# Two spectral-and-MLP layers on one core: rest transposes moved to other banks, stores moved to another queue, and four small changes of order

## The chip, the cores and the metric

The kernel runs on one core of a Trainium2 chip. The core has five engines that run beside one another, each in its own program order: TensorE (PE in the profile, its weight loads PEld), VectorE (DVE), ScalarE (ACT), GpSimd (POOL) and SyncE (SP). They meet at semaphores. TensorE writes its sums into PSUM, which has eight banks here; an engine that wants to write into a bank waits for the readers of what was there. Transfers between the chip's memory and the core's on-chip memory are issued by an engine's queue: almost all here by SP's, a few by ACT's. A queue takes its transfers in order, and one that waits for its data holds back those behind it.

The metric is the device time of one execution in microseconds (us), lower is better. A difference of 0.2%, which is 5.4 us here, is about what a measurement of this kernel can tell from no change.

## The reference, cut to what matters

```python
# S = 2048 tokens, D = 576, F = 4608, float32, one batch
def A(x):                      # Fourier mixing
    a = einsum("bsd,ed->bse", x, dft_hid_re)      # along the hidden axis
    b = einsum("bsd,ed->bse", x, dft_hid_im)
    return einsum("ts,bse->bte", dft_seq_re, a) - einsum("ts,bse->bte", dft_seq_im, b)

def B(x):                      # channel MLP
    y = layernorm(x)
    h = gelu(einsum("bsd,df->bsf", y, w1) + b1)   # tanh form
    return einsum("bsf,fd->bsd", h, w2) + b2

for layer in range(2):
    x = x + A(layernorm(x))
    x = x + B(layernorm(x))
```

## The kernel before, in words

**Arithmetic.** Every product of two float32 matrices is made from three passes: each factor is kept as a high part (a rounded copy, written by ACT) and a low part (the rest, a subtraction), and TensorE adds high x high, high x low and low x high. In the profile R is a buffer of such parts and A one of plain float32. On top of that, block products go by a scheme with 7 products of 2 x 2 blocks in place of 8 (numbered 1 to 7, taken in the order 1, 6, 2, 5, 7, 3, 4), which needs sums of blocks before (DVE and POOL) and sums of products after (DVE reads the banks).

**Stages of a layer.** `Sequence` applies the transform along the tokens first. `fill` loads two tiles of x at a time (a pair p), takes their norm (BN_STATS, BN_AGGR, a short chain on POOL), and makes high and low parts. While pairs arrive, `first_mms` multiplies them with the first two row blocks, and `first_post` writes those two blocks of results (ACT, L603) and stores them into `uv_mid` (L605). Then steps (t, i) go over the other row blocks: `load_block` loads a block of coefficients (`in_cs`), `sums` and `low` prepare it on DVE, `high` on ACT, `mms` multiplies. `Hidden` applies the transform along the hidden axis, one half of the tokens at a time, normalizes, and turns the blocks of the result by transposes on TensorE into y (`turn_y`). `mlp` follows for the same half: 18 rounds `inner(q)` make 512 columns each of gelu(y w1 + b1) and split them, and 9 rounds `outer(g)` multiply by w2 and add the products into the result, in two sides of four and three products.

**What sets the order.** The order is written by hand: generators hand out work between the products, and each engine keeps the order in which its instructions were written. In `mlp` three mechanisms matter here:

- The eight steps that finish a round q (its last gelu, then seven high parts on ACT and seven low parts) are put into a list of tasks; `outer` takes from it through `work(n)`, one task at two of three slots (L1276), or at every slot in the last two rounds g.
- `advance` counts slots, and at due numbers written in a list (L1129 for the last group of w2) makes the high part, then the low part and the next difference, of one block of w2.
- `store` (L1367) writes finished tiles of the result, two at a time, while the last products still run.

**What stands around turn_y.** Its last call is interleaved with the first products of `inner(0)`: four steps after the first product, one after the second, one after the third. Its first four steps transpose 14 blocks of 128 columns into a pair of banks that `space()` hands out; its last two transpose 7 rest blocks of 96 columns (L982) into the free halves of the four banks in which `inner(0)` gathers its products. A bank's half can be written once the gelu (L1174) that reads the bank is through.

The instructions of helpers carry the helper's line: L205 every product, L195 every addition, L198 every subtraction, L192 almost every transfer, L201 the high part in a split.

## Time and profile before

| what | value |
|---|---|
| three runs | 2705.21, 2706.81, 2708.84 us; median 2706.81 |
| the profiled execution's own time | 2707.04 us |
| its span in the trace | 2705.2 us |
| granted TensorE clock, mean | 0.999 |
| busy: TensorE | 2669.1 us of the span |
| busy: VectorE | 1769.2 us (65%) |
| busy: ScalarE | 1101.6 us (41%) |
| busy: GpSimd | 794.3 us (29%) |
| transfers | 544.92 MB, 201 GB/s in the mean |

The span is that of one profiled execution; what the device time has beyond it (1.8 us) lies before the first and after the last instruction of the trace. Start times in the rows count from the span's start. In rows of the timeline the columns are start, length, engine, line, operation, what it writes and reads, how many instructions of that kind in a row, and in brackets how long the engine stood idle before the first and what ended that.

### The profile page before, as it was taken

How to read it: one execution, taken by the hardware profiler on the slowest of the kernel's cores; microseconds unless marked ns; L12 is line 12 of the kernel's file. 1: busy time of each engine (PE TensorE's matmuls, PEld its weight loads, DVE VectorE, ACT ScalarE, POOL GpSimd, SP SyncE). 2: the span in 40 equal slices, each digit the busy share in tenths (PEclk: the TensorE clock that was granted, in tenths of full speed). 3: DMA queues.
4: the chain of work that ended last, by engine and by line, in shares of the span. 5: the costliest groups of instructions: out<-in, count | busy, mean ns of one | idle time of the engine just before them, and what ended most of it. 6: DMA issues, size and time to landing. Idle time of an engine off the chain costs nothing. (4 is left out here: it accounts for less than half of the span.)

```text
span 2705.2 us, 45278 instructions
## 1 busy us (share of the span) xinstructions
PE 2669.1 (99%) x17540; PEld 2500.6 (92%) x17540; DVE 1769.2 (65%) x2573; ACT 1101.6 (41%) x1841; POOL 794.3 (29%) x740
## 2 busy tenths in 40 slices
PE   9999999999999999999999999999999999999998
PEld 9999999888888988998899999998999899898988
DVE  8888866778776565556676666466555546555555
ACT  6555544544443343333354333343333314433331
POOL 6223234544442432222250000142222234322222
PEclk9999999999999999999999999999999999999999
DMA  4777775777777466666454333546666673666664
GB/s 173 264 261 245 242 260 183 262 266 272 263 268 290 151 180 194 195 217 207 153 194 141 124 121 123 192 138 193 194 193 196 190 273 110 208 192 194 192 194 151
DMA packets 209286, 544.92 MB, mean 201 GB/s; under 512 B 22048, under 2 KB 56864, under 8 KB 208928
## 3 DMA queue, kind: packets, MB, share of 16 engines
q1 hardware_dynamic: 197408, 515.48, 58.9%
q10 hardware_dynamic: 11664, 26.55, 2.5%
q8 instruction: 139, 2.28, 0.3%
q14 instruction: 75, 0.61, 0.1%
HBM read 429.87 MB, written 114.72 MB: 201 GB/s over the span
## 5 line engine op out<-in xcount | busy, mean ns | idle before, releaser
L205 PE MATMUL bank<-R 128*128 128x288 f32 (+2 forms) x16972 | 2612.4, 315 | 17.9 <-DVE A L195 9.8
L205 PEld LDWEIGHTS bank<-R 128*128 128x128 f32 x16972 | 2438.6, 189 | 182.0 <-DVE A L195 22.4
L195 DVE TENSOR_TENSOR A<-bank,A 128x576 f32<-128x576 f32 (+3 forms) x808 | 567.9, 709 | 551.2 <-PE bank L205 471.3
L198 POOL TENSOR_TENSOR R<-A,R 128x512 fp32r<-128x512 f32 (+1 forms) x288 | 375.6, 1315 | 913.6 <-ACT R L1235 873.1
L198 DVE TENSOR_TENSOR R<-A,R 128x1024 fp32r<-128x1024 f32 (+9 forms) x521 | 494.5, 972 | 57.2 <-ACT R L643 23.6
L195 POOL TENSOR_TENSOR A<-A 128x576 f32<-128x576 f32 (+2 forms) x102 | 138.0, 1355 | 568.0 <-ACT A L683 365.4
L1174 ACT ACTIVATE bank<-bank,b1t 128x512 f32<-128x512 f32 (+1 forms) x224 | 144.9, 647 | 369.6 <-DVE bank L195 242.7
L1235 ACT ACTIVATE R<-A 128x512 fp32r<-128x512 f32 x288 | 176.0, 628 | 272.4 <-DVE A L198 118.2
L198 POOL TENSOR_TENSOR A<-A 128x384 f32<-128x384 f32 (+3 forms) x156 | 198.2, 1273 | 248.7 <-DVE R L198 128.1
L643 ACT ACTIVATE R<-A 128x1024 fp32r<-128x1024 f32 x196 | 204.6, 1052 | 120.2 <-DVE A L198 97.7
L195 DVE TENSOR_TENSOR bank<-bank,A 128x512 f32<-128x512 f32 (+1 forms) x228 | 152.2, 670 | 144.7 <-PE bank L205 143.8
L198 DVE TENSOR_TENSOR R<-bank,R 128x512 fp32r<-128x512 f32 (+1 forms) x328 | 204.9, 639 | 52.1 <-ACT R L201 46.9
L198 DVE TENSOR_TENSOR A<-A 128x1024 f32<-128x1024 f32 (+3 forms) x134 | 140.9, 1058 | 4.6 <-DVE R L198 0.4
L1201 ACT ACTIVATE A<-bank 128x512 f32<-128x512 f32 (+1 forms) x76 | 43.8, 576 | 234.9 <-PE bank L205 231.4
L1235 ACT ACTIVATE R<-bank 128x512 fp32r<-128x512 f32 x216 | 121.2, 595 | 29.8 <-PE bank L205 29.7
L198 DVE TENSOR_TENSOR A<-bank,A 128x512 f32<-128x512 f32 x144 | 97.9, 680 | 0.0
L201 ACT ACTIVATE R<-bank 128x512 fp32r<-128x512 f32 (+1 forms) x112 | 49.4, 491 | 85.3 <-PE bank L856 79.1
L1174 ACT ACTIVATE A<-bank,b1t 128x512 f32<-128x512 f32 (+1 forms) x76 | 50.6, 666 | 66.0 <-DVE bank L195 66.0
L685 DVE SCALAR_TENSOR_TENSOR A<-A 128x288 f32<-128x288 f32 x28 | 16.0, 572 | 83.3 <-POOL A L195 83.3
L275 ACT ACTIVATE R<-A 128x256 fp32r<-128x256 f32 x126 | 52.0, 413 | 44.3 <-DMA w_parts<-R 18.4
L249 ACT ACTIVATE A<-A,moments 128x576 f32<-128x576 f32 x58 | 48.6, 862 | 48.2 <-POOL moments L230 19.8
L276 ACT ACTIVATE R<-A,power,middle 128x128 fp32r<-128x128 f32 x126 | 60.8, 482 | 0.0
(67 smaller groups left out, 629.2 us busy)
## 6 DMA issues: line engine op xcount, KB each, us to landing
R<-w_parts SPq DMA_DIRECT2D x504, 320.0 KB, 3.4
R<-w_parts SPq DMA_DIRECT2D x189, 576.0 KB, 3.7
A<-in_cs SPq DMA_DIRECT2D x112, 512.0 KB, 4.1
w_parts<-R SPq DMA_DIRECT2D x63, 576.0 KB, 5.1
w_parts<-R ACTq DMA_DIRECT2D x81, 320.0 KB, 3.2
uv_mid<-A SPq DMA_DIRECT2D x32, 576.0 KB, 3.1
w_parts<-R SPq DMA_DIRECT2D x45, 320.0 KB, 4.3
A<-in_w SPq DMA_DIRECT2D x72, 192.0 KB, 4.8
```

What stands on the lines that cost most here:

```text
L195: engine.tensor_tensor(dst, a, b, op=op)
L198: engine.tensor_tensor(dst, a, b, op=OP.subtract)
L201: nc.scalar.activation(hi, src, AF.Copy)
L205: nc.tensor.matmul(o, a, b, start=start, stop=stop, skip_group_check=True)
L249: nc.scalar.activation(dst, src, AF.Identity, bias=mv[:, 4:5], scale=mv[:, 3:4])
L275: nc.scalar.activation(t[:, 1:4:2], src[:, 0:3:2], AF.Copy)
L276: nc.scalar.activation(t[:, 2], src[:, 1], AF.Identity, bias=power[:, 2:3], scale=middle)
L643: nc.scalar.activation(self.cells[t, i](2, NP, P)[:, 0], self.source(t, i), AF.Copy)
L685: nc.vector.scalar_tensor_tensor(uv[:, 1, 0], p7, -1.0, u, op0=OP.mult, op1=OP.subtract)
L1174: nc.scalar.activation(dst, src, AF.Gelu_apprx_tanh, bias=bias(f))
L1201: nc.scalar.activation(up, o, AF.Copy)
L1235: nc.scalar.activation(H[q, k](2, TC)[:, 0], src, AF.Copy)
```

## The change

Eight edits, in the order of the program:

1. **Start.** In layer 0 the BN_STATS of the first tile of pair 1 are taken by DVE directly after pair 0 is normalized, ahead of pair 0's low parts; `stats_of_pair` then takes those of the second tile only.
2. **First stores.** `first_post` issues its store into `uv_mid` on ACT's queue, in both layers, two stores each.
3. **Buffers in `run`.** The second result block is taken from the buffers of x in place of a new one, and `hidden.reserve` follows both.
4. **turn_y.** The 7 rest transposes go into one more pair of banks from `space()`, all after the first 14 products of 7 matmuls each, and are read by two copies (4 and 3 blocks) in place of three. Each layer and half has one such place: four in all.
5. **Due list.** The last group of w2 gets other due numbers; the list is used in layer 0, first half.
6. **Round q = 0.** In the first `mlp`, two low parts go from POOL to DVE.
7. **Rate of tasks.** The second side of `outer(7)` takes two tasks in three slots in place of one per slot, so two tasks fall behind it. Four places.
8. **Last stores.** In the last half, every second store of a tile of the result goes to ACT's queue.

```diff
@@ stats_of_pair @@
+    def tile_stats(st, src, which):
+        for h in which:
             nc.vector.bn_stats(st[:, h // 2, h % 2 * 6:h % 2 * 6 + 6], src[:, h, :])
+
+    def stats_of_pair(src, plain, later, begun=None):
+
+        st, mv = begun or moments()
+        tile_stats(st, src, (2, 3) if begun else range(4))
@@ fill @@
+                if p == 0 and not self.early:
+                    self.begun = moments()
+                    tile_stats(self.begun[0], self.x[1], (0, 1))
                 if p < 2 and not self.early:
                     self.low_left(p)
@@ first_post @@
-            dma(uvd[t], out(2 * D))
+            nc.scalar.dma_start(uvd[t], out(2 * D))
@@ run @@
             self.first_post(0, outs[0])
+            outs.append(next(b for b in self.xs if b.at != raw.at))
+            self.xs.remove(outs[1])
             for _ in self.pieces:
                 pass
-            if outs[0].at < UV_AT + 4 * D:
-                outs.pop().free()
-            hidden.reserve()
-            steps = self.steps
-            outs.append(A.alloc(2 * D))
-            self.first_post(1, outs[-1])
+            self.first_post(1, outs[1])
             for out in outs:
                 clock[0] += 1
                 out.free()
+            hidden.reserve()
+            steps = self.steps
@@ turn_y @@
+            o = space()
             for i0 in (0, 4):
-                ov = bank[:, i0 // 2:i0 // 2 + 2, 2 * P:].rearrange("p a (b t) -> p a b t", t=P)
+                ov = o[:, i0 // 4].rearrange("p (i t) -> p i t", t=P)
                 ni = min(4, 7 - i0)
                 for i in range(ni):
-                    nc.tensor.transpose(ov[:96, i // 2, i % 2], es(7, 96)[:, blocks[i0 + i] - 1], ident)
-                for i in range(0, ni, 4 if ni == 4 else 2):
...
+                    nc.tensor.transpose(ov[:96, i], es(7, 96)[:, blocks[i0 + i] - 1], ident)
+                nc.scalar.activation(y[:96, i0:i0 + ni, 2, at], ov[:96, :ni], AF.Copy)
                 yield
@@ end of the hidden stage @@
-        for n in (4, 1, 1):
+        for n in (4, 0, 2):
@@ due list @@
-                        list(zip((5, 7, 7, 8, 9, 10, 11, 12, 12, 13, 13, 14), six + five + three + seven + four + two)))
+                        list(zip((6, 8, 9, 10, 10, 11, 12, 13, 13, 14, 14, 14), six + five + three + seven + four + two)))
@@ step @@
-                    sub(nc.vector if n < 4 or first and q == NQ - 1 else nc.gpsimd, h[:, 1], src, h[:, 0].bitcast(F32))
+                    sub(nc.vector if n < 4 or first and (q == NQ - 1 or q == 0 and n < 6) else nc.gpsimd, h[:, 1], src, h[:, 0].bitcast(F32))
@@ outer @@
-                work(slot[0] % 3 < 2 or g >= last - 1)
+                work(slot[0] % 3 < 2 or g == last - 1 and side == 0)
@@ store @@
-                dma(to[t * P:(t + 1) * P, :].rearrange("p (e d) -> p e d", e=2), xv[:, :, j])
+                queue = nc.scalar if layer and half and j % 2 else nc.sync
+                queue.dma_start(to[t * P:(t + 1) * P, :].rearrange("p (e d) -> p e d", e=2), xv[:, :, j])
```

**turn_y, TensorE and ScalarE.** The rows below are TensorE's around the last call of `turn_y`, before and then with the change. L973 and L979 are the 14 transposes of whole blocks, L982 and L989 the rest transposes, L205 the products of `inner(0)`.

```order
L205 MATMUL bank<-R 128x256 x35
L973 MATMUL bank<-ident,A 128x128 x14
L205 MATMUL bank<-R 128x256 x7
L982 MATMUL bank<-ident,A 96x128 x4
L205 MATMUL bank<-R 128x256 x7
L982 MATMUL bank<-ident,A 96x128 x3
L205 MATMUL bank<-R 128x256 x49
```

```order
L205 MATMUL bank<-R 128x256 x35
L979 MATMUL bank<-ident,A 128x128 x14
L205 MATMUL bank<-R 128x256 x14
L989 MATMUL bank<-ident,A 96x128 x7
L205 MATMUL bank<-R 128x256 x49
```

The three rest transposes that stood behind the second seven products and the four ahead of them now stand together behind both. ScalarE's rows at the same place, before and then with the change: L201 the high parts of the whole blocks, L1174 (L1176 with the change) the gelus, L985 and L988 (L990) the copies of the rest blocks.

```order
L201 ACTIVATE R<-bank 128x2x2x128 x3
L201 ACTIVATE R<-bank 128x2x128
L1174 ACTIVATE bank<-bank,b1t 128x256
L985 ACTIVATE R<-bank 96x4x128
L1174 ACTIVATE A<-bank,b1t 128x256
L988 ACTIVATE R<-bank 96x2x128
L988 ACTIVATE R<-bank 96x128
L1201 ACTIVATE A<-bank 128x256
```

```order
L201 ACTIVATE R<-bank 128x2x2x128 x3
L201 ACTIVATE R<-bank 128x2x128
L1176 ACTIVATE bank<-bank,b1t 128x256
L1176 ACTIVATE A<-bank,b1t 128x256
L990 ACTIVATE R<-bank 96x4x128
L990 ACTIVATE R<-bank 96x3x128
L1203 ACTIVATE A<-bank 128x256
```

The copy of the first four rest blocks moved from ahead of the second gelu to behind it.

**First stores, SyncE.** A piece of the difference of SyncE's rows in layer 0, from the loads of coefficients around the first results on (`in_cs`):

```order
 L192 DMA A<-in_cs 128x1024 x4
 L192 DMA A<-in_x 128x576 x2
-L192 DMA uv_mid<-A 128x1152 x2
 L192 DMA A<-in_cs 128x1024 x3
 L192 DMA A<-in_w 128x384 x4
```

The three loads of coefficients now stand directly behind the last loads of x, with no store ahead of them; the two stores stand on ScalarE, each behind the four copies of L603.

**Last group of w2, VectorE.** VectorE's rows in the second side of `outer(8)` of layer 0, first half, before and then with the change. L195 with A<-bank,A reads a finished product (evacuation); L198 with 128x2x288 is a low part of w2 and with A<-A 128x576 the difference that follows it.

```order
L195 TENSOR_TENSOR A<-bank,A 128x576
L198 TENSOR_TENSOR R<-A,R 128x512 x2
L198 TENSOR_TENSOR R<-A,R 128x2x288
L198 TENSOR_TENSOR A<-A 128x576
L195 TENSOR_TENSOR A<-bank,A 128x576
L198 TENSOR_TENSOR R<-A,R 128x2x288
L195 TENSOR_TENSOR A<-bank,A 128x576 x2
```

```order
L195 TENSOR_TENSOR A<-bank,A 128x576
L198 TENSOR_TENSOR R<-A,R 128x512 x2
L195 TENSOR_TENSOR A<-bank,A 128x576
L198 TENSOR_TENSOR R<-A,R 128x2x288
L198 TENSOR_TENSOR A<-A 128x576
L195 TENSOR_TENSOR A<-bank,A 128x576 x2
L198 TENSOR_TENSOR R<-A,R 128x2x288
```

The evacuation moved ahead of the low part and the difference of block 6.

More of the change, by code (lines that the diff above doesn't have):

```diff
@@ L231, in stats @@
         return mv
-    def stats_of_pair(src, plain, later):
-        st, mv = moments()
-        for h in range(4):
+    def tile_stats(st, src, which):
+        for h in which:
             nc.vector.bn_stats(st[:, h // 2, h % 2 * 6:h % 2 * 6 + 6], src[:, h, :])
+    def stats_of_pair(src, plain, later, begun=None):
+        st, mv = begun or moments()
+        tile_stats(st, src, (2, 3) if begun else range(4))
         for h in range(2):
@@ L325, in __init__ @@
             self.Z, self.parts, self.b12, self.v, self.x, self.mv = [None] * NP, {}, {}, {}, {}, {}
+            self.begun = None
             self.ready, self.closed, self.wish = 0, False, list(range(NP))
@@ L524, in norm_stats @@
             if p not in self.mv:
-                self.mv[p] = stats_of_pair(self.x[p], p == 0 and not self.early, p > 2)
+                self.mv[p] = stats_of_pair(self.x[p], p == 0 and not self.early, p > 2, self.begun if p == 1 else None)
         def normalize(self, p):
```

5 lines of the change are left out of this document (removed).

## The prediction

> **What bounds the kernel now.** I read the page's busy table first, then the waits of TensorE, then the timeline around each wait that the change touches. The first row below is of the busy table; the others are of the waits of TensorE (line, what it waited for, total us, times, longest).
>
> ```profile
> PE 2669.1 (99%) x17540; PEld 2500.6 (92%) x17540; DVE 1769.2 (65%) x2573; ACT 1101.6 (41%) x1841; POOL 794.3 (29%) x740
> ```
>
> ```profile
> PE bank L205 <- DVE A L195: 9.8, 7, 2.4
> PE bank L982 <- ACT A L1174: 6.5, 4, 1.6
> PE bank L982 <- ACT bank L1174: 3.6, 4, 0.9
> ```
>
> TensorE works in 2669.1 of 2705.2 us. The change removes no matmul, so it can gain only from the 36 us in which TensorE stands, or from time in which it runs at a lower clock. What is to be seen: the four places of turn_y hold 6.5 + 3.6 = 10.1 us, and waits for VectorE's readings of banks 9.8 us in 7 places.
>
> **The sum, part by part.** It is made against the profiled execution's 2707.04 us (span 2705.2), which lies 0.23 above the median of 2706.81. Gains count positive.
>
> *turn_y, four places.* The timeline at the first one:
>
> ```profile
> 452.80 1.08 PE L205 MATMUL bank<-R 128*128 128x256 f32 x7
> 455.00 0.42 PE L982 MATMUL bank<-ident,A 128*96 128x128 f32 x2 [0.90 <-ACT bank L1174]
> 455.52 0.60 ACT L985 ACTIVATE R<-bank 96x512 fp32r<-96x512 f32 x1 [0.57 <-PE bank L982]
> 457.36 0.47 ACT L1174 ACTIVATE A<-bank,b1t 128x256 f32<-128x256 f32 x1 [1.24 <-DVE bank L195]
> 457.89 0.53 PE L982 MATMUL bank<-ident,A 128*96 128x128 f32 x3 [1.63 <-ACT A L1174]
> 458.18 1.08 PE L205 MATMUL bank<-R 128*128 128x256 f32 x7
> ```
>
> Now: the third rest transpose waits 0.90 for a gelu, the last three wait 1.63 for the next gelu, and the 49 products start at 458.18. With the change the 14 products run through and the 7 transposes need no gelu, since their banks are free: from 452.80 on, 14 x 0.154 (1.08 / 7) and 7 x 0.18 (0.53 / 3) end at about 456.2. The 49 products begin, but their seventh needs the rest blocks in y, and that copy (0.60) now stands on ScalarE behind the gelu that ends at 457.83, which itself waits for VectorE. So it ends at 458.4. The wait is not removed, it moves behind six products: at 458.4 six stand done where before it was one or two. Gain 4.5 x 0.125 to 0.154, about 0.5 a place, 2.0 in four. Ends: 0, if VectorE's addition ahead of the gelu slips by as much; 2.5 a place if the copy came without the gelu, which ScalarE's order excludes. I take the low value, since the gelu's row names VectorE as what it waits for, and VectorE's order there is unchanged.
>
> *Start.*
>
> ```profile
> 7.95 2.56 DVE L198 TENSOR_TENSOR R<-A,R 128x1024 fp32r<-128x1024 f32 x3 [0.37 <-ACT R L538]
> 10.43 1.53 DVE L237 BATCH_NORM_STATS2 moments<-A 128x6 f32<-128x288 f32 x4
> 18.30 0.92 PE L205 MATMUL bank<-R 128*128 128x288 f32 x5 [0.69 <-DVE R L198]
> ```
>
> Two BN_STATS cost 1.53 / 2 = 0.77. VectorE idles 0.37 ahead of the low parts, which the moved pair fills; the low parts start 0.40 later, the chain of pair 1 behind them 0.37 earlier. TensorE waits once more for those low parts, then at 18.30 for the end of pair 1's chain: 0.37 gained there, if the stages up to 69.67 (where it next stands) hand it on. Ends: minus 0.4 (only the delay stays) and plus 0.7 (the whole wait).
>
> *First stores.* The timeline of the first results, two windows (engine columns, clock, DMA share, GB/s), and SyncE's waits from 50 to 110:
>
> ```profile
> 67.08 1.30 ACT L603 ACTIVATE A<-bank 128x288 f32<-128x288 f32 x4
> 68.24 1.08 ACT L643 ACTIVATE R<-A 128x1024 fp32r<-128x1024 f32 x1
> 68.40 0.33 SPq L192 DMA_DIRECT2D uv_mid<-A  x1
> 68.82 2.50 SPq L192 DMA_DIRECT2D A<-in_cs  x3
> 69.67 10.05 PE L205 MATMUL bank<-R 128*128 128x288 f32 x74 [0.43 <-ACT A L675]
> 76.85 1.23 DVE L195 TENSOR_TENSOR A<-A 128x1024 f32<-128x1024 f32 x1 [3.25 <-DMA A<-in_cs]
> 80.52 9.78 PE L205 MATMUL bank<-R 128*128 128x288 f32 x72 [0.80 <-DVE R L198]
> 90.96 0.40 PE L205 MATMUL bank<-R 128*128 128x288 f32 x1 [0.65 <-DVE R L198]
> ```
>
> ```profile
> 55.00:60.00 5.00, 5.00 (x40) 5.00 (x39) 4.94 (x5) 3.84 (x8) 0.03 (x1) 1.00 0.00 0
> ...
> 70.00:75.00 5.00, 5.00 (x40) 5.00 (x39) 3.60 (x4) 2.99 (x4) 0.00 (x0) 1.00 0.99 316
> ```
>
> ```profile
> SPq L192 <- ACT A L603: 32.3, 2, 24.5
> ```
>
> SyncE stands 32.3 us for the copies of L603 with loads of coefficients behind the stores. Nothing is moved at 55 to 60 (share 0.00), everything at 70 to 75 (0.99). VectorE then waits 3.25 for a load and TensorE 0.80 and 0.65 for low parts. With the stores on ScalarE the next loads stand behind loads of x alone and can go while the DMA engines are empty; then VectorE's sums come up to 3.25 earlier and both stalls go: 1.45. For layer 1 I count nothing. The price is on ScalarE, whose store waits for its own copies (end 68.38) before the next ACTIVATE, now at 68.24:
>
> ```profile
> 88.64 1.10 ACTq L290 DMA_DIRECT2D w_parts<-R  x2
> 89.55 0.40 ACT L275 ACTIVATE R<-A 128x256 fp32r<-128x256 f32 x1
> ```
>
> Two issues take 1.10, yet the next ACTIVATE starts 0.19 before their end. So ScalarE loses between 0.14 (68.38 - 68.24) and 0.14 + 0.55; I take 0.28, nearer the low end by that row. It delays L675, for which TensorE waits at 69.67. Start and price together: 0.37 - 0.28 = 0.1. The part: 1.45 + 0.1 = 1.55; ends -1.1 (nothing but delay: 0.4 and 0.69) and 2.0.
>
> [...]
>
> *Round q = 0.*
>
> ```profile
> 474.87 5.06 POOL L198 TENSOR_TENSOR R<-A,R 128x512 fp32r<-128x512 f32 x4
> 480.61 1.66 PE L205 MATMUL bank<-R 128*128 128x512 f32 x6 [0.78 <-ACT A L1201]
> 851.66 1.95 DVE L198 TENSOR_TENSOR R<-A,R 128x512 fp32r<-128x512 f32 x3
> ```
>
> The wait of 0.78 ends behind four low parts on POOL; with two fewer (2.5 us) POOL is done in time and it goes. But VectorE's first low part stands ahead of an addition for which TensorE waits. One takes 0.65 on VectorE (1.95 / 3, the last row, later in the program), and 1.27 on POOL (5.06 / 4), which I take as the upper end for VectorE beside a busy POOL. Part of it falls into VectorE's idle time: a stall of 0.5, nearer the row of VectorE itself. The gain is 0.3; ends -0.5 (0.78 - 1.27) and 0.8 (no stall).
>
> *Rate of tasks.*
>
> ```profile
> 822.87 1.32 PE L205 MATMUL bank<-R 128*128 128x288 f32 x8 [0.94 <-DVE A L195]
> ```
>
> ```profile
> 830.00:836.00 6.00, 6.00 (x27) 4.91 (x27) 2.72 (x5) 2.59 (x5) 0.00 (x0) 1.00 0.76 231
> ```
>
> In layer 0, first half, TensorE waits 0.94 in this side for VectorE's reading of a bank, with VectorE working without a break ahead of it. One task fewer takes a low part (0.65) or more out: 0.85, between 0.65 and 0.94. The other three places show no stall: 0. The two moved tasks land in the next round, where VectorE is busy 2.72 of 6.00 us (the window); if that cover were gone, one low part of 0.7 would come in a place.
>
> *Due list.*
>
> ```profile
> 853.64 0.76 DVE L198 TENSOR_TENSOR A<-A 128x576 f32<-128x576 f32 x1
> 854.32 0.75 DVE L195 TENSOR_TENSOR A<-bank,A 128x576 f32<-128x576 f32 x1
> 855.21 9.07 PE L205 MATMUL bank<-R 128*128 128x288 f32 x55 [2.27 <-DVE A L195]
> ```
>
> ```profile
> 856.00:858.00 2.00, 2.00 (x11) 2.00 (x11) 0.68 (x2) 0.00 (x0) 0.00 (x0) 0.53 1.01 415
> ...
> 1340.00:1342.00 2.00, 0.00 (x0) 0.00 (x0) 2.00 (x3) 0.00 (x0) 1.29 (x1) 1.00 0.81 269
> 1342.00:1344.00 2.00, 1.65 (x12) 1.65 (x13) 1.56 (x3) 0.30 (x1) 0.00 (x0) 1.00 0.11 46
> ```
>
> The evacuation at 854.32 stands behind block 6's low part (the third of the row at 851.66) and a difference (853.64). With the change it follows the second low part, at about 852.9, and TensorE goes on near 853.75, 1.45 earlier. But its second side of products then needs block 6's low part, done only at 854.3: some 0.5 comes back. Gain 1.0, between 0 and 1.5. What is late next is block 2's high part, which waits for a store; I count nothing for it, and one low part (0.65) where it comes late.
>
> Behind this stall the granted clock is 0.53 for a while (the window 856 to 858; the two windows below it belong to the rivals). The 55 matmuls took 9.07 where 72 take 9.78 (the row at 80.52): 55 x 0.136 = 7.5, so 1.6 went to the clock. With the stall cut to pieces below 1 us I take it as not coming: +1.6, ends 0 and 1.6.
>
> [...]
>
> *Last stores.*
>
> ```profile
> 2696.09 5.49 SPq L192 DMA_DIRECT2D out<-A  x8
> ```
>
> ```profile
> 2699.00:2700.00 1.00, 0.00 (x0) 0.00 (x0) 0.32 (x1) 0.00 (x0) 0.00 (x0) 1.00 1.08 381
> ```
>
> The eight stores move at 381 GB/s with a share of 1.08, so their bytes and not their issue set the end: 0, within 0.3 either way. The buffers of the third edit add no wait that I can find: 0.
>
> Sum: 2.0 + 1.55 + 0.3 + 0.85 + 1.0 + 1.6 = 7.3, so 2707.04 - 7.3 = 2699.7.
>
> **The rivals.**
>
> *The waits come back one engine on.* turn_y gives 0 (the gelu waits for VectorE either way), round 0 loses 0.5, half of the coefficient loads' gain stays (0.8) and one side with moved tasks loses 0.7. For it: three of these stalls end on VectorE, which has no gap there. Against it: the rows at 76.85 and 853.64 name work that is plainly moved away. Time: 2707.04 - (0 + 0.8 - 0.5 + 0.85 - 0.7 + 1.0 + 1.6) = 2704.0. That is no change.
>
> *The low clock stays, here or elsewhere.* From 1340 to 1342 TensorE stood for all of 2.00 us, and the clock was 1.00 there and in the two us behind it, while 2.27 us at 853 brought it down; so it hangs on more than the length, and a shift of a few us can bring it to a stall that the change leaves alone. Time: 2699.7 + 1.6 = 2701.3, on the bound. For it: the clock has fallen once in this trace, after a stall shorter than 2.4 us. Against it: the longest stall that the change touches is the one that it cuts. [...]
>
> *ScalarE is held by its store.* If the queue kept ScalarE until the store has landed (3.1 us, the row below), L675 and the low parts behind it would come late by that, in both layers:
>
> ```profile
> uv_mid<-A SPq DMA_DIRECT2D x32, 576.0 KB, 3.1
> ```
>
> Against it stands the row at 89.55, an ACTIVATE 0.9 after the first issue. At 3.1 it costs 6.2 against gains of 7.6 elsewhere (7.3 without my 0.28): 2705.6. It decides from a landing of 6.4 us on: 2 x 6.4 - 7.6 = 5.2, and 2707.04 + 5.2 is 0.2% over the median. At 8 us: 2707.04 + 16 - 7.6 = 2715.4.
>
> **How the numbers follow.** The forecast as summed 0.48; the clock 0.2; waits back one engine on 0.25; ScalarE held, or another loss of that size, 0.07. Predicted: 2699.7. Low end 2697: turn_y 1.0 a place (+2.0) and 0.5 from round 0. High end 2704.5: the second kind of outcome. Below 2701.4 (0.2% under 2706.81; 0.2% is about what a measurement of this kernel can tell from no change): 0.42 of the forecast and 0.11 of the clock's, with 0.02 of the third: 0.55. Slower than 2712.2: 0.07. The rest, 0.38.
>
> **What would show it.** In the trace after: the 49 products of turn_y's places stand after their sixth, for the copy of rest blocks, at most 1.3 us; no stall of 0.9 and 1.6 on L1174 there. The loads of coefficients before 60 us, and no stall at 80 and 90. No 0.94 in the second side of outer(7). One stall below 1 us and a second at block 6 in outer(8), with the clock 1.00 behind. The last stores still at 381 GB/s. The prediction is wrong if a stall stands in the inner rounds behind the moved tasks, if L675 is late, or if the clock falls somewhere that it did not.

## The result, and the profile after

The changed kernel takes 2699.61 us, the median of 7 runs (2697.9 to 2701.31). The kernel before, measured again beside it, takes 2708.84 us (7 runs, 2705.21 to 2711.87). The ratio is 0.997 with a 95% interval of 0.996 to 0.998: faster by 0.2 to 0.4%. The profiled execution of the changed kernel took 2700.23 us, with a span of 2698.4, against 2707.04 and 2705.2 before: 6.8 us less. The forecast was 2699.7, faster. The number came out; the runs below show that several of its terms did not, and that they made up for one another.

First the busy row of the page after, then the waits of TensorE after (line, what it waited for, us in total, times, longest):

```profile
PE 2668.4 (99%) x17540; PEld 2505.5 (93%) x17540; DVE 1771.6 (66%) x2575; ACT 1101.7 (41%) x1837; POOL 789.6 (29%) x738
```

```profile
PE bank L205 <- ACT R L990: 8.7, 4, 2.2
PE bank L205 <- DVE A L195: 6.4, 7, 2.0
PE bank L205 <- DVE R L198: 2.3, 4, 0.8
...
PE bank L205 <- ACT A L682: 0.9, 1, 0.9
```

The four places of turn_y held 10.1 us of waits in eight stalls; they now hold 8.7 us in four. Waits for VectorE's readings fell from 9.8 to 6.4. L682 (L675 before), one wait, grew from 0.4 to 0.9.

The timeline after at the first place of turn_y, then two windows behind it (busy time of TensorE, its weight loads, VectorE, ScalarE and GpSimd, then the granted clock, the share of the DMA engines and GB/s):

```profile
451.18 1.92 PE L205 MATMUL bank<-R 128*128 128x256 f32 x14
...
452.94 0.93 PE L989 MATMUL bank<-ident,A 128*96 128x128 f32 x7
...
453.62 0.96 PE L205 MATMUL bank<-R 128*128 128x256 f32 x6
...
455.75 0.47 ACT L1176 ACTIVATE A<-bank,b1t 128x256 f32<-128x256 f32 x1 [2.42 <-DVE bank L195]
456.12 0.96 ACT L990 ACTIVATE R<-bank 96x512 fp32r<-96x512 f32 x2
456.76 5.48 PE L205 MATMUL bank<-R 96*128 96x256 f32 x31 [2.18 <-ACT R L990]
```

```profile
456.00:458.00 2.00, 1.24 (x6) 1.24 (x7) 0.05 (x1) 1.47 (x4) 0.00 (x0) 0.72 0.58 202
458.00:460.00 2.00, 2.00 (x11) 2.00 (x11) 0.42 (x1) 0.00 (x0) 0.00 (x0) 0.50 0.65 175
```

Six of the 49 products run, then TensorE stands 2.18 us for the copy of the rest blocks, which stands behind the gelu, which waits 2.42 for VectorE. That is the forecast's mechanism to the product. Two things the forecast did not have. The stall is 2.18 long where it said at most 1.3: the 14 products and 7 transposes ahead of the 49 take 2.44 (451.18 to 453.62) and not 3.4. And the stall has a second cost: behind it the clock is at half (0.50 from 458 to 460 us).

The first stores after, in the timeline, and the window from 70 to 75 us:

```profile
36.03 35.04 SPq L192 DMA_DIRECT2D A<-in_cs  x3
...
68.11 0.33 ACTq L612 DMA_DIRECT2D uv_mid<-A  x1
68.48 1.06 ACT L650 ACTIVATE R<-A 128x1024 fp32r<-128x1024 f32 x1 [0.40 <-ACT A L610]
...
69.89 20.36 PE L205 MATMUL bank<-R 128*128 128x288 f32 x152 [0.93 <-ACT A L682]
```

```profile
70.00:75.00 5.00, 5.00 (x38) 5.00 (x39) 4.06 (x5) 3.18 (x4) 0.00 (x0) 1.00 0.68 239
```

The loads of coefficients begin at 36.03 in place of 68.82, the DMA engines are at 0.68 in place of 0.99 from 70 to 75, and TensorE runs 20.36 us without a stall where it stood 0.80 and 0.65. ScalarE waits 0.40 for its own copies at the store.

Round 0, the second side of outer(8) and the end of the span, in the timeline after:

```profile
474.50 0.71 DVE L198 TENSOR_TENSOR R<-A,R 128x512 fp32r<-128x512 f32 x1
...
474.65 7.66 PE L205 MATMUL bank<-R 128*128 128x512 f32 x32 [0.56 <-DVE bank L195]
...
850.97 0.74 DVE L195 TENSOR_TENSOR A<-bank,A 128x576 f32<-128x576 f32 x1
...
851.86 0.37 PE L205 MATMUL bank<-R 128*128 128x288 f32 x1 [0.83 <-DVE A L195]
...
852.43 3.80 PE L205 MATMUL bank<-R 128*128 128x288 f32 x26 [0.20 <-DVE R L198]
...
2689.29 3.86 SPq L1372 DMA_DIRECT2D out<-A  x4
2689.30 3.97 ACTq L1372 DMA_DIRECT2D out<-A  x4
```

```profile
854.00:856.00 2.00, 2.00 (x17) 1.97 (x16) 1.62 (x3) 0.00 (x0) 0.00 (x0) 1.00 1.01 417
...
2693.00:2696.00 3.00, 0.00 (x0) 0.00 (x0) 0.00 (x0) 0.00 (x0) 0.00 (x0) 1.00 1.08 378
```

The stall of 0.78 in round 0 is gone and one of 0.56 stands ahead of it. The stall of 2.27 in outer(8) is now 0.83 and 0.20, with the clock at 1.00 behind. The last stores leave on two queues and move 378 GB/s, as they did on one (381).

**Where the time went, stretch by stretch.** Both kernels run 17540 matmuls in TensorE's order, alike but for the rest transposes in turn_y. So the n-th start of one can be set against the n-th of the other. The table gives the length of stretches in us, worked out from the two traces; products are counted from 0.

```
products       place                                before   after   difference
0-110          start                                18.25    17.95   -0.30
110-490        to behind the wait for L675 / L682   50.96    51.49   +0.53
490-640        first stores, loads of coefficients  21.83    19.84   -1.99
3380-3540      turn_y 1 and round 0                 34.41    34.91   +0.50
5400-5500      outer(7), first of four places       15.76    14.76   -1.00
5600-5760      outer(8)                             26.11    24.01   -2.10
6380-6500      turn_y 2                             22.64    23.65   +1.01
12100-12240    turn_y 3                             25.49    24.69   -0.80
15120-15260    turn_y 4                             26.77    27.79   +1.02
8440-8490, 14180-14230, 17185-17235
               outer(7), the other three places     22.39    20.82   -1.57
all others     (differences of up to 1.0 each)                       -2.1
```

The sum is -6.8, the difference of the spans.

### The profile page after: what moved, and what is told of

It reads as the page before. It is cut to its first block, busy times and chain, and to the rows that moved or that the text cites. A ratio compares the mean times of both kernels' runs of the same rounds, so it can differ in the third digit from the quotient of the medians.

```text
span 2698.4 us, 45272 instructions
## 1 busy us (share of the span) xinstructions
PE 2668.4 (99%) x17540; PEld 2505.5 (93%) x17540; DVE 1771.6 (66%) x2575; ACT 1101.7 (41%) x1837; POOL 789.6 (29%) x738
## 5 line engine op out<-in xcount | busy, mean ns | idle before, releaser
L205 PE MATMUL bank<-R 128*128 128x288 f32 (+2 forms) x16972 | 2612.6, 315 | 21.9 <-ACT R L990 8.7
L205 PEld LDWEIGHTS bank<-R 128*128 128x128 f32 x16972 | 2442.9, 189 | 182.6 <-DVE A L195 18.7
L195 DVE TENSOR_TENSOR A<-bank,A 128x576 f32<-128x576 f32 (+3 forms) x808 | 568.5, 710 | 546.6 <-PE bank L205 469.4
L198 POOL TENSOR_TENSOR R<-A,R 128x512 fp32r<-128x512 f32 (+1 forms) x286 | 373.3, 1315 | 912.9 <-ACT R L1237 871.5
L198 DVE TENSOR_TENSOR R<-A,R 128x1024 fp32r<-128x1024 f32 (+9 forms) x523 | 496.3, 972 | 57.7 <-ACT R L650 24.4
L195 POOL TENSOR_TENSOR A<-A 128x576 f32<-128x576 f32 (+2 forms) x102 | 136.9, 1346 | 565.5 <-ACT A L690 367.4
L1176 ACT ACTIVATE bank<-bank,b1t 128x512 f32<-128x512 f32 (+1 forms) x224 | 144.9, 647 | 373.8 <-DVE bank L195 244.0
L198 POOL TENSOR_TENSOR A<-A 128x384 f32<-128x384 f32 (+3 forms) x156 | 197.4, 1267 | 250.8 <-DVE R L198 106.6
L195 DVE TENSOR_TENSOR bank<-bank,A 128x512 f32<-128x512 f32 (+1 forms) x228 | 152.3, 670 | 143.7 <-PE bank L205 142.8
L198 DVE TENSOR_TENSOR R<-bank,R 128x512 fp32r<-128x512 f32 (+1 forms) x328 | 205.3, 640 | 51.5 <-ACT R L201 46.8
L198 DVE TENSOR_TENSOR A<-A 128x1024 f32<-128x1024 f32 (+3 forms) x134 | 140.9, 1058 | 4.5 <-DVE R L198 0.2
L198 DVE TENSOR_TENSOR A<-bank,A 128x512 f32<-128x512 f32 x144 | 98.1, 681 | 0.0
L201 ACT ACTIVATE R<-bank 128x512 fp32r<-128x512 f32 (+1 forms) x112 | 49.4, 491 | 81.1 <-PE bank L862 74.8
L1176 ACT ACTIVATE A<-bank,b1t 128x512 f32<-128x512 f32 (+1 forms) x76 | 50.6, 666 | 70.3 <-DVE bank L195 70.2
```

The costliest lines, as they stand in the source:

```text
L195: engine.tensor_tensor(dst, a, b, op=op)
L198: engine.tensor_tensor(dst, a, b, op=OP.subtract)
L201: nc.scalar.activation(hi, src, AF.Copy)
L205: nc.tensor.matmul(o, a, b, start=start, stop=stop, skip_group_check=True)
L1176: nc.scalar.activation(dst, src, AF.Gelu_apprx_tanh, bias=bias(f))
```

## The experiments

Each kernel below has one profile, and its time is a median of 4 to 8 runs. Stretches are read as in the table above. The kernels ran in four groups, each on a chip of its own, and the changed kernel was not run again beside them; the kernel before was, with medians of 2707.77 to 2709.33 in the four. So a difference of 1.6 us between medians of different groups says nothing, and one below 5.4 us is weak. The clock that an execution lost is summed over windows of 2 us (1 less the granted clock, times 2).

### One edit undone: turn_y

The changed kernel with the lines of turn_y and the steps (4, 1, 1) of the kernel before.

```diff
-            o = space()
             for i0 in (0, 4):
-                ov = o[:, i0 // 4].rearrange("p (i t) -> p i t", t=P)
+                ov = bank[:, i0 // 2:i0 // 2 + 2, 2 * P:].rearrange("p a (b t) -> p a b t", t=P)
...
-        for n in (4, 0, 2):
+        for n in (4, 1, 1):
```

> The changed kernel with turn_y and its steps as before (edit 4 undone). Theory of the clock: the one stall of 2.18 us that edit 4 makes of two shorter ones brings the granted clock to half for 3.4 us in three of the four places, and each costs 1.5 us; without edit 4 the stalls of 0.9 and 1.6 us are back, no low clock stands behind them, and the kernel takes about 2.4 us less than the changed one: 2697.2. Rival, the forecast's term: edit 4 is worth 2.0 us and the low clock comes from somewhere else and stays: 2701.6, with a low clock near 456, 954 or 2290.

It took 2702.99 us (8 runs, 2699.96 to 2705.64), 3.4 more than the changed kernel: the opposite of my theory, and on the side of the forecast's term, though below 5.4. Waits of TensorE and windows at two of the places:

```profile
PE bank L988 <- ACT A L1180: 6.5, 4, 1.6
PE bank L988 <- ACT bank L1180: 3.6, 4, 0.9
```

```profile
952.00:954.00 2.00, 1.65 (x8) 1.63 (x9) 0.12 (x1) 0.84 (x3) 0.00 (x0) 0.50 0.00 0
...
1806.00:1808.00 2.00, 1.54 (x8) 1.53 (x9) 0.23 (x1) 0.95 (x3) 0.00 (x0) 0.50 0.00 0
```

Behind the pair of stalls of before the clock came down as well: here at two of its four places (0.50 in both windows), where the profiled execution of the kernel before had none. That execution had been a lucky one. Compared with it alone, edit 4 loses 1.0 us in three places; compared with this execution of the same lines, it gains 1.6 in all. The four profiles that have the old lines and the six that have the new ones put the gain at 1.4 us in the mean (0.3, 0.3, 1.4 and -0.7 by place).

### One step earlier: the rest transposes at (4, 2, 0)

```diff
-        for n in (4, 0, 2):
+        for n in (4, 2, 0):
```

The 7 transposes and both copies now stand ahead of the second of the first products and ahead of the second gelu.

> The changed kernel with the steps of turn_y as (4, 2, 0): all 7 rest transposes and both copies stand ahead of the second of the first products and of the second gelu. Theory of the clock and of ScalarE's order: the seventh of the 49 products no longer waits for the gelu; TensorE stands about 0.7 us at the transposes in place of 2.18, no low clock follows, so (2.18 - 0.7) x 4 + 1.5 x 3 = 10 us less than the changed kernel: about 2689.5. Rival: the long wait only moves to the next product, because VectorE has no gap there (its low parts and additions run from 451.8 to 456.0): stalls of about 2 us stay, 2699.

It took 2690.62 us (4 runs, 2689.7 to 2692.07), 9.0 below the changed kernel; the ratio to the kernel before is 0.9934 (0.9917 to 0.995). TensorE at the first place:

```profile
452.62 1.04 PE L989 MATMUL bank<-ident,A 128*96 128x128 f32 x7 [0.35 <-DVE R L198]
453.41 2.76 PE L205 MATMUL bank<-R 128*128 128x256 f32 x21
456.54 3.74 PE L205 MATMUL bank<-R 128*128 128x256 f32 x29 [0.37 <-ACT A L1203]
```

The stall of 2.18 is now 0.35 and 0.37, at all four places, and the clock behind them stays at 1.00. So the products waited for the gelu through ScalarE's order alone, and VectorE did not bind there. The rival is out. In this one line lies about as much as in all eight edits (9.0 and 9.2 us).

### One edit undone: the due list

```diff
-                        list(zip((6, 8, 9, 10, 10, 11, 12, 13, 13, 14, 14, 14), six + five + three + seven + four + two)))
+                        list(zip((5, 7, 7, 8, 9, 10, 11, 12, 12, 13, 13, 14), six + five + three + seven + four + two)))
```

> The changed kernel with the old due numbers of the last group of w2 (edit 5 undone). Theory: the stall of 2.27 us in outer(8) of the first half is back, with the half clock behind it: 2.1 us more than the changed kernel, 2701.7. [...]

The medians do not tell the kernels apart (2700.15, 7 runs, against 2699.61). In the trace the stall is back, and the clock behind it is not low but at 1.00 (how this stall lies against the steps of the clock is shown below under "How often the clock fell"):

```profile
852.04 2.25 PE L205 MATMUL bank<-R 128*128 128x288 f32 x15 [2.26 <-DVE A L195]
```

```profile
852.00:854.00 2.00, 1.96 (x15) 1.99 (x16) 1.30 (x3) 0.00 (x0) 0.00 (x0) 1.00 1.04 422
854.00:856.00 2.00, 2.00 (x18) 2.00 (x17) 2.00 (x4) 0.00 (x0) 0.00 (x0) 1.00 1.04 411
```

Products 5600 to 5760 take 24.58 here, 24.01 with the new list and 26.11 before. So of the 2.10 gained there, 0.57 is the stall and 1.53 the clock of that one execution.

### One edit undone: the first stores

```diff
-            nc.scalar.dma_start(uvd[t], out(2 * D))
+            dma(uvd[t], out(2 * D))
```

> The changed kernel with the first results' stores back on SyncE's queue (edit 2 undone). Theory: loads of coefficients wait behind the stores again; stalls of 0.8 and 0.65 us near 80 and 90 us are back and the wait for L682 (L675 before) at 69 us shrinks by 0.3 to 0.5: about 1.1 us more, 2700.7. Rival, that a second queue saves issue time alone: no stall comes back, within 0.3 us of the changed kernel up to 110 us.

The medians are level (2699.81, 6 runs), as 1.1 us is below what they tell. In the trace:

```profile
69.13 10.07 PE L205 MATMUL bank<-R 128*128 128x288 f32 x74 [0.42 <-ACT A L682]
79.70 9.83 PE L205 MATMUL bank<-R 128*128 128x288 f32 x72 [0.49 <-DVE R L198]
90.13 2.15 PE L205 MATMUL bank<-R 128*128 128x288 f32 x14 [0.60 <-DVE R L198]
```

Products 490 to 640 take 21.54 in place of 19.84 (1.70 more), products 110 to 490 take 50.94 in place of 51.49 (0.55 less): edit 2 is worth 1.15 net, as this run's expectation had it. (Over all profiles products 490 to 640 take 21.54 to 21.88 in the five with the stores on SyncE and 19.83 to 19.86 in the eight others, so the 1.70 is the low end of 1.7 to 2.0.) By the rival no stall near 80 and 90 us would have come back; both did (0.49 and 0.60).

### One edit alone: the buffers

The kernel before with edit 3 alone.

```diff
             self.first_post(0, outs[0])
+            outs.append(next(b for b in self.xs if b.at != raw.at))
+            self.xs.remove(outs[1])
             for _ in self.pieces:
                 pass
-            if outs[0].at < UV_AT + 4 * D:
-                outs.pop().free()
-            hidden.reserve()
-            steps = self.steps
-            outs.append(A.alloc(2 * D))
-            self.first_post(1, outs[-1])
+            self.first_post(1, outs[1])
...
+            hidden.reserve()
+            steps = self.steps
```

> The kernel before with edit 3 alone (the second result block taken from the buffers of x, the hidden stage's buffers reserved behind it). The changed kernel's products run some 2% faster in stretches of the second halves and of layer 1 where the order of work is the same in both (235 ns against 230 ns a product of 512 columns; 1.6 us in all, and 0.4 us early in layer 1). Theory of the addresses: edit 3 moves buffers, so these stretches are faster here too: 136.0 us for products 7000 to 7800, where the kernel before took 136.6, and 26.45 for 9200 to 9400, where it took 26.84. Rival, another edit or that one execution: 136.6 and 26.84 stay. For the clock, which fell once in the profiled execution of the kernel before: the theory of chance says that it falls at one to four of its long stalls here.

2707.68 us (8 runs), ratio 0.9996 (0.9985 to 1.0007): no change. Products 7000 to 7800 take 136.26, between the two values; in the thirteen profiles they take 136.00 to 136.62, whatever the kernel. Products 9200 to 9400 take 26.45 here, but also in the next run, which has the old buffers; the 26.84 belongs to the one execution of before. The theory of addresses falls, and with it some 2 us of the difference of the first two profiles are differences of executions. What makes the pace differ I could not settle. One rival is on record: products 15260 to 17150 take 323.5 to 323.9 us in the four profiles of this group (buffers, rate of tasks, round 0, last stores), which ran on one chip, and 322.9 to 323.0 in the seven of the other experiments, which ran on three others. On which chips the first two profiles ran is not recorded.

The clock came down at three places of turn_y, in outer(8), and in the stage near 1340 us: 10.2 us lost, against 1.7 in the profiled execution of before. One window of each place:

```profile
458.00:460.00 2.00, 1.59 (x8) 1.57 (x9) 0.18 (x1) 0.90 (x3) 0.00 (x0) 0.50 0.11 38
858.00:860.00 2.00, 2.00 (x10) 2.00 (x10) 0.29 (x1) 0.00 (x0) 0.00 (x0) 0.50 1.01 408
960.00:962.00 2.00, 2.00 (x12) 2.00 (x11) 0.00 (x0) 0.80 (x3) 0.00 (x0) 0.50 0.03 8
2298.00:2300.00 2.00, 1.77 (x9) 1.75 (x10) 0.00 (x0) 0.72 (x3) 0.00 (x0) 0.50 0.00 0
```

### One edit alone: the rate of tasks

```diff
-                work(slot[0] % 3 < 2 or g >= last - 1)
+                work(slot[0] % 3 < 2 or g == last - 1 and side == 0)
```

> The kernel before with edit 7 alone (the rate of tasks in the second side of outer(7)). Theory: the forecast saw one of four places; the stall of 0.94 us in layer 0, first half, goes, and in the other three places four waits of TensorE's weight loads for VectorE's readings of banks, about 0.13 us each on the products' pace, go too: 0.9 + 3 x 0.55 = 2.5 us less in these four places, read from the trace. Rival, the forecast's term: 0.85 us in the first place and nothing in the others. The 2% of pace: 136.6 us for products 7000 to 7800 if it does not hang on this edit, 136.0 if it does.

2707.63 us (8 runs), ratio 0.9991 (0.998 to 1.0002). In the trace the four places take 7.43, 6.90, 6.90 and 6.94 us (50 products each), where the kernel before took 8.42, 7.48, 7.47 and 7.44: 2.64 in all, 1.65 of it in the three places that the forecast gave nothing. The weight loads show why, first in the kernel before, then with this edit alone, at the fourth place:

```profile
2646.36 1.62 PEld L205 LDWEIGHTS bank<-R 128*128 128x128 f32 x12 [0.26 <-DVE A L195]
...
2648.22 1.61 PEld L205 LDWEIGHTS bank<-R 128*128 128x128 f32 x12 [0.24 <-DVE A L195]
...
2650.08 3.08 PEld L205 LDWEIGHTS bank<-R 128*128 128x128 f32 x23 [0.25 <-DVE A L195]
```

```profile
2646.88 1.51 PEld L205 LDWEIGHTS bank<-R 128*128 128x128 f32 x11
2648.65 6.42 PEld L205 LDWEIGHTS bank<-R 128*128 128x128 f32 x48 [0.26 <-DVE A L195]
```

TensorE waits 0.24 to 0.26 us for VectorE at every twelfth product, in its weight loads, and the row of the products shows no idle time there at all. With one task fewer VectorE is ahead, and two of the three waits go.

### One edit undone: round 0

```diff
-                    sub(nc.vector if n < 4 or first and (q == NQ - 1 or q == 0 and n < 6) else nc.gpsimd, h[:, 1], src, h[:, 0].bitcast(F32))
+                    sub(nc.vector if n < 4 or first and q == NQ - 1 else nc.gpsimd, h[:, 1], src, h[:, 0].bitcast(F32))
```

> The changed kernel with the two low parts of round 0 back on POOL (edit 6 undone). Theory: the stall of 0.56 us at 474 us goes and the one of 0.78 near 478 is back, with the slower products beside it; the stretch of products 3450 to 3540 takes 0.3 to 0.6 us more. Rival, that VectorE's new work costs as much as POOL's saves: the stretch within 0.2 us.

2701.22 us (8 runs). The wait behind POOL is back:

```profile
474.95 5.04 POOL L198 TENSOR_TENSOR R<-A,R 128x512 fp32r<-128x512 f32 x4
480.02 0.60 ACT L1203 ACTIVATE A<-bank 128x512 f32<-128x512 f32 x1 [3.52 <-POOL R L198]
480.68 1.66 PE L205 MATMUL bank<-R 128*128 128x512 f32 x6 [0.83 <-ACT A L1203]
```

Products 3500 to 3540 take 10.41 in place of 9.22 (1.19 more), products 3380 to 3500 take 25.07 in place of 25.69 (0.62 less; the clock fell in both executions, so this number is the weaker one). Edit 6 is worth 0.57. The other profiles bear it out: products 3450 to 3540, behind the low clock, take 22.78 to 22.89 in the five with these parts on POOL and 22.31 to 22.52 in the eight with them on DVE.

### One edit undone: the last stores

```diff
-                queue = nc.scalar if layer and half and j % 2 else nc.sync
+                queue = nc.sync
```

> The changed kernel with all last stores on SyncE's queue (edit 8 undone). Theory of the bytes: the end of the span behind the last product stays at 6.7 us, within 0.3, since 380 GB/s are moved to the end. Rival, that one queue's issues (5.5 us for eight) hold the last stores: 1 us or more longer.

2700.37 us (6 runs). The span ends 6.7 us behind the last product here, in the changed kernel and in the kernel before. So the issues do not set it; with the DMA share at 1.08 and 381 GB/s from 2690 to 2693 us, the bytes do. Edit 8 is worth nothing.

### turn_y alone, at (4, 2, 0)

The kernel before with the new lines of turn_y, at the steps of the second experiment, and nothing else.

```diff
+            o = space()
             for i0 in (0, 4):
...
-        for n in (4, 1, 1):
+        for n in (4, 2, 0):
```

> The kernel before with the moved rest transposes alone, at the steps (4, 2, 0). Theory: the stalls of 0.9 and 1.6 us in four places shrink to about 0.35 and 0.37, which is 1.8 us a place or 7.2 in all, and the half clock, which followed 7 of 16 such pairs so far at 1.3 to 2.5 us each, follows none: another 2.8 us in the mean. About 10 us below the kernel before: 2699.3 against 2709.3. Rival, that the low clock only moves to the next long stall: 7.2 us, 2702.1, with the clock at 0.5 somewhere within 20 us behind the four places.

2698.81 us (4 runs, 2697.41 to 2699.88); ratio 0.9961 (0.9946 to 0.9976). The four places show stalls of 0.36 and 0.37 and a clock of 1.00. So 10 us, as expected, from one of the eight edits in another order. Read off the four places, the two profiles at (4, 2, 0) lie 9.9 below the mean of the four with the old lines.

### A stall of middle length

The changed kernel with the steps (4, 1, 1): four rest transposes early, three late.

```diff
-        for n in (4, 0, 2):
+        for n in (4, 1, 1):
```

> The changed kernel with the steps of turn_y as (4, 1, 1): the first four rest transposes and their copy ahead of the second gelu, the last three and theirs behind it. Theory: product 13 of the 49 waits for the last copy, one stall of 1.0 to 1.4 us a place in place of 2.18; if the clock falls by the length of one stall, four stalls of this size bring it down nowhere: 4 x 0.9 + 4 x 0.6 x 1.5 = 7.2 us below the changed kernel, 2692.4. Rival, that any stall near 1 us can bring it down with a chance that grows with its length: a low clock behind one or two of the four, 2694 to 2695.

2692.59 us (4 runs, 2691.82 to 2693.79). The last copy keeps TensorE waiting 0.80 us a place, and the clock falls at none:

```profile
PE bank L205 <- ACT R L990: 3.2, 4, 0.8
```

This is what the theory of one stall's length said, with a stall shorter than I had put it; one execution cannot exclude a small chance.

### One edit undone: the start

```diff
-                if p == 0 and not self.early:
+                if False:
                     self.begun = moments()
```

> The changed kernel with pair 1's BN_STATS all in one place again (edit 1 undone). In all profiles so far with the first stores on ScalarE, products 0 to 490 take 69.2 to 69.7 us, whether the start was early or late; with the stores on SyncE and edit 1 (e4) they take 68.7. Theory: ScalarE, held behind the copies of L610 for its store, sets when TensorE goes on at 69 us, and what edit 1 gains at 18 us is waited away there: without it products 0 to 110 take 18.25 to 18.5 us in place of 17.95, and products 0 to 490 still 69.2 to 69.7. Rival, the forecast: 0.37 us come back, 69.8 or more.

2699.80 us (8 runs), level with the changed kernel. Products 0 to 490 take 69.49, against 69.44, and products 0 to 110 take 18.01, against 17.95: in these two executions edit 1 shows next to nothing, and the wait at 69 us is the same. But a wait at 17 us is back:

```profile
16.96 0.40 PE L205 MATMUL bank<-R 128*128 128x288 f32 x1 [0.49 <-ACT R L557]
...
69.92 2.29 PE L205 MATMUL bank<-R 128*128 128x288 f32 x15 [0.89 <-ACT A L682]
```

Two executions are too few for a term of this size, and the other profiles tell more. The five kernels without edit 1 all have this wait of 0.5, the eight with it do not. Products 0 to 110 take 18.01 to 18.53 without it (18.3 in the mean), and 17.71 to 17.95 in six of the eight with it (17.8); in the other two the clock fell at 11 us, and they take 18.60 and 18.69. Nor is the gain waited away at 69 us, as my theory had it: with the stores on ScalarE products 110 to 490 take 51.46 to 51.51 whether the start took 17.71 or 18.01, and with them on SyncE 50.93 to 50.96 whether it took 17.73 or 18.53. Only the two late starts are caught up in part (51.0). So edit 1 is worth some 0.5 us where the clock does not fall at the start, 0.3 with the two in which it did.

### How often the clock fell

Thirteen profiles, counted by the windows in which the granted clock is below 0.9, at the places that had a long stall:

```
stall (us)                     place                    clock fell    executions x places
0.9 and 1.6, 1.2 us apart      turn_y, steps of before     7          16
2.2                            turn_y, changed            15          24
0.80                           turn_y, (4, 1, 1)           0           4
0.36 and 0.37, 3.5 us apart    turn_y, (4, 2, 0)           0           8
2.3                            outer(8), old due list      3           5
0.8 and 0.2                    outer(8), new due list      0           8
2.0 and 1.0 to 2.4             near 1335 us                8          13
0.3 and 1.3 or 1.4             start, 9 to 11 us           2           2
0.2 to 1.4, a single one       start, 9 to 11 us           0          11
```

A fall is one stretch of 3.413 us at half clock (1.7 us lost), two in a row in 6 of the 35 counted, and in turn_y and outer(8) it cost the stretch in which it stood 1.3 to 2.5 us.

The traces also show where the falls lie. The four low stretches of the changed kernel ahead of its last product begin at 456.86, 955.21, 1334.09 and 2289.82 us, each is 3.413 us long by the trace's record of the granted clock, and their starts are 146, 111 and 280 such lengths apart. In each of the twelve profiles with more than one low stretch, all changes of the granted clock lie whole multiples of 3.413 us apart. So each execution can be laid out on one grid of steps of 3.413 us, and where that grid lies against the program differs by execution. Adding up TensorE's idle time in every step that ran at full clock, in all thirteen profiles: the step behind is at half clock in 28 of 28 cases with 1.95 us or more, in 7 of 29 with 1.47 to 1.93, and in none below that. In the changed kernel the stall of 2.18 lies within one step at three places of turn_y, and the next step is at half clock; at the third place a boundary at 1805.13 cuts it into 1.05 and 1.13, and the clock stays at 1.00. In the kernel before, the stall of 2.27 in outer(8) lies within the step from 852.70 to 856.11, and the clock falls at 856.11. In the run with the old due list the boundary at 851.20 cuts the stall of 2.26 into 1.41 and 0.85, and the clock stays. Why the cases between 1.47 and 1.93 differ is open.

## Why the prediction came out, and which of its steps did not

- **turn_y, 2.0 us.** The mechanism was right to the product: the wait moved behind six products and was not removed, and by places without a low clock the gain is 0.5 (22.17 in one execution of the new lines against 22.64), 0.5 and 0.8. Two steps failed. The stall was put at 1.3 at most and is 2.18: for the 14 products and 7 transposes the step took the lengths of whole rows (1.08 / 7 and 0.53 / 3), 3.4 us in all, but in the trace after they take 2.44, so TensorE stands about 1 us longer for a copy that came when forecast. And the step priced the stalls without the clock. Behind the one stall of 2.2 us it fell 15 times in 24, so against the profiled execution of before the term was a loss of 2.2 us (three times +1.0, once -0.8), not a gain of 2.0. Behind the old pair it fell as well, 7 times in 16; by the mean over all profiles the gain is 1.4. The medians lie 3.4 apart, and the counts do not explain the rest of that. The upper end of 2.5 us a place, which the forecast excluded by ScalarE's order, is what the order (4, 2, 0) comes near: 1.7 to 2.0 a place, against places of the old lines without a low clock.
- **Start, 0.37, and the price on ScalarE, 0.28.** Given 0.1 net. Measured: edit 1 0.3 between the two profiles and 0.3 to 0.5 over all of them, handed on to 69 us as the forecast had it; the price 0.55, twice its size. The wait at 18.30, which the forecast would shorten, stayed at 0.69 or 0.70 where it stands; what went is the one of 0.5 ahead of it.
- **Loads of coefficients, 1.45.** 1.70 by the run with the edit undone; with the price of 0.55 the net is 1.15 against 1.17 forecast (1.45 - 0.28). Right, by two errors of 0.3 that cancel.
- **Round 0, 0.3.** 0.57. The new stall came where the forecast put it and at its size (0.56 against 0.5); the slower products beside it, which were gained back too, were not counted.
- **Rate of tasks, 0.85.** 2.64. The first place was right (1.0). The sentence "The other three places show no stall: 0" failed: I had read the products' waits only, and the loss stood in the weight loads'.
- **Due list, 1.0 and 1.6 for the clock.** 0.57 and 1.53 against that execution. The stall in two pieces (0.83 and 0.20) came as described and is 1.2 shorter, but the stretch only 0.57, less than the 1.0 of the step. The 1.6 is real only in executions in which the clock falls there, 3 of 5. That it would not fall behind pieces below 1 us was the author's estimate; behind the pieces of 0.8 and 0.2 it fell in 0 of 8 profiles.
- **Last stores and buffers, 0.** Right.
- **The rivals.** The low clock elsewhere, given 0.2, is what happened: it left outer(8) and came at three places of turn_y and near 1335 us. Where the grid of 3.413 us lies against the program differs among the profiles, and the same stall of 2.2 us in turn_y was followed by half clock in 15 of 24 cases; 1.95 us of idle time or more in one step were followed by it every time, 28 of 28. The rival that the waits come back one engine on, given 0.25, is out for round 0, which gained, for the loads, whose two stalls went, and for the moved tasks: products 5500 to 5600, behind them, take 18.11 us before and 18.12 after. The rival that ScalarE is held until its store has landed is out: the next ACTIVATE starts 0.37 behind the issue (68.11 and 68.48). Of the three signs of being wrong that the prediction named, two came: the wait for L682 (L675) grew from 0.43 to 0.93, and the clock fell where it had not.
- **The sum.** 7.3 forecast, 6.8 between the two profiled executions. By the runs the terms are -2.2 (turn_y), 0.3 (start), 1.15 (first stores), 0.57, 2.64 and 2.10, in all 4.6; of the other 2.2 us, 2.0 are the pace of three stretches (products 7000 to 7800, 9200 to 9400 and 15260 to 17150), which the profiles tie to no edit, and the rest is not assigned. So turn_y was 4.2 too high, start and first stores 0.1 and the due list 0.5 too high, the rate 1.8 and round 0 0.3 too low, and the rest is the luck of the two executions. Between medians the gain is 9.2, since the profiled execution of before stood 1.8 below the median of its seven runs and that of the changed kernel 0.6 above its own. That the number was hit was luck and says little for the terms.

## What to carry to other kernels

Where a stall of about 2 us recurs, its price can be more than its length: here the clock fell behind 26 of 42 stalls of 2.0 to 2.3 us, and in turn_y and outer(8) a fall cost 1.3 to 2.5 us more. Look at the granted clock behind such a stall, and take more than one execution before a price is put on it, since where the grid of 3.413 us cut the stall differed here from one to the next. Read the waits of the weight loads beside those of the matmuls; here a loss of a quarter of a microsecond, three times in a row, showed only there. And where a copy waits behind an activation that it does not need, move it ahead by one step before anything else is tuned (9.0 us here).

## What was not expected of the hardware

- The granted clock fell to 0.5 behind stalls of 2.0 to 2.3 us in 26 of 42 cases, behind two of 0.9 and 1.6 us that 1.2 us of work part in 7 of 16, and behind single stalls of 0.8 us or less in none of the places counted above. The profile of the kernel before lost 1.7 us to it, those of two kernels that are nearly the same 10.2 us each; the seven runs of before spread over 6.7 us (2705.21 to 2711.87), and 25 later ones over 10.2 (2704.09 to 2714.32). Each fall began at a boundary of the execution's own grid of steps of 3.413 us.
- In the stage near 1335 us, where VectorE is what TensorE waits for, a low clock cost little: with it products 8580 to 8720 take 24.4 to 26.2 us, without it 24.3 to 25.7.
- The same products in the same order ran 0.3% to 1.5% apart in stretches (over thirteen profiles, products 15260 to 17150: 322.9 to 323.9 us; products 9200 to 9400: 26.44 to 26.84), not by kernel but by execution or by chip. The cause stays open.
